# Gated Hedgehog attention with a SwiGLU gate: four FFN blocks computed ahead instead of six, and what lies around the hand-over from attention to FFN

## The chip, the cores and the metric

The kernel runs on one core of a Trainium2 chip, as one launch. The metric is the device time of the whole program in microseconds, the median of several runs. Beside these runs stands one profiled execution, from which all rows of the profile are taken; its span is the time from its first to its last recorded instruction.

The core has a matrix engine (TensorE, PE in the profile, with its weight loads as PEld), a vector engine (VectorE, DVE), a scalar engine (ScalarE, ACT), a general engine (GpSimd, POOL) and a queue engine that only issues transfers (SyncE, SP). Each executes its own instructions strictly in the order in which they stand. Work on different engines is tied together by semaphores: an instruction that waits holds up all that stand behind it on the same engine.

## What is computed

All data are float32. With 2048 rows, width 576, 32 heads of 18 and an FFN width of 4608, the reference is, cut to what matters:

```python
def A(x):                                     # linear attention with a learned feature map
    q, k, v = heads(x @ wqkv)
    pq, pk = q @ w_phi, k @ w_phi             # per head, 18 x 18
    phi_q = concat(softmax(pq), softmax(-pq)) # 36 features a head
    phi_k = concat(softmax(pk), softmax(-pk))
    kv, z = phi_k.T @ v, phi_k.sum(rows)
    return (phi_q @ kv) / (phi_q @ z + 1e-6) @ wo

def B(x):                                     # SwiGLU FFN
    return (silu(x @ w_gate) * (x @ w_up)) @ w_down

xn = layernorm(x)
out = x + A(xn) * silu(B(xn))
```

## The kernel before

**Arithmetic.** Each operand is split into a rounded part and a remainder, and a product is three matmuls: high by high, high by low, low by high. The split is the helper `split` (L57 to L59): a cast on ACT, then a subtraction on DVE that waits for it. The width of 576 is cut into chunks of 128 with a shared tail chunk, so that one 128 x 512 tile of a product with full depth takes 14 matmuls of 512 columns (`xw`, L82 to L92).

**Stages.** The order on each engine is set by a scheduler that places instructions by priority and by its own estimate of when operands are there; the program gives the sequence and marks some work as urgent (`tc.high_priority`) or as not before another instruction (`tc.issue_after`).

1. The rows are normalised and transposed into eight tiles `XB[i][j]`: for each half `i` of the rows two blocks of 512 rows by two halves of the width (L148 to L201). The feature map is folded into the query and key weights (`fold`, L210 to L220); the folded query weights are `QH` and `QL` in the pool `const`.
2. Key stage (L347 to L380): for 16 row tiles the key and value products, the softmaxes, and the sums `kv`. In the background `spread_out` (L325 to L343) forms sums and differences of the four tiles of each half of x and stores them in `sum_dram`, for the later FFN.
3. Query stage (L402 to L500): for eight blocks of 256 rows, `q_tile` (query product, softmaxes, denominators; the last DVE product of a row tile is kept in `last_e`), then a block later `numer` (five groups of heads: transposes into `pt`, a split to `ph` and `pl`, six matmuls into `po`, a split to `oh` and `ol`) and `project` (four quarters of 15 matmuls of 288 columns into `p`, each copied to `so` on ACT, L483; the store of `so` to `s_dram` from SP, L485). `po` and `p` have one buffer each. `tails` (L414 to L427) prepares the small tail weights of the FFN.
4. FFN. The F width is cut into 36 blocks of 128. For the first `EARLY` blocks, gate and up products are made plainly (`early_tile`, L110 to L121: for a half and a block 2 tiles x 2 weights x 14 matmuls = 56) and stored in `h_dram`. They stand behind the attention in the program (L502 to L505), and the scheduler sets their matmuls between those of the attention. The last early block is computed after the attention (L858 and after); between its two halves the sums of x are loaded into the tiles of the second half of x (`operands`, L511 to L530).
   The other blocks use a Strassen-like scheme (`gate_up`, L591 to L632): seven products of seven matmuls for a half and block, 49, from the operands `xo` and from weights that `gate_up_weights` (L532 to L564) loads into `ld`, combines on POOL (`ts`), splits into `w2` and `w1`, and stores for the second half of the rows in `w_dram`; `wt` holds the tails.
   The down product takes pairs of blocks, two pairs together, again in seven products (`strassen`, L730 to L809): `prep` (L799 to L806) splits the rows `h` to `hh` and the down weights to `dw`; part 0 are the products 1 and 7, part 1 are 4, 5, 6, 2, 3. The matmuls of the down product (`three`, L669) are placed between those of `gate_up` by `fill`. For the first group of the first half, the down weights of one pair come from `first_rows`, loaded into a part of `acc` (L860 to L862).
   `units` (L828 to L833) is the order of the 36 blocks for each half: an early block is put in at every fourth place and read back from `h_dram` (`stored`).

**Buffers.** Pools are laid on a stack: the FFN's weight pool `fw` (L507) takes the place that the attention's pools leave. A pool without more said waits, with its first use, for the pools whose place it takes; with `reuse_waits="tile"` each tile waits for just those that lay on its own bytes. `fp` and `fq` have that already.

**Queues.** Nearly all transfers are issued from SP, in one order; a transfer that has to wait for its data holds up those behind it.

Of the kernel before, what the change touches and what calls it, by code (L numbers as in the profile page):

```python
# [9 lines left out]
F32 = mybir.dt.float32  # L10
F32R = mybir.dt.float32r
# [5 lines left out]
S, D, H, DH, F = 2048, 576, 32, 18, 4608  # L17
P = 128
NT = S // P
BT = 512  # L20
# [3 lines left out]
HALF = D // 2  # L24
# [2 lines left out]
GROUPS = [(g * GW, min(GW, D - g * GW)) for g in range((D + GW - 1) // GW)]  # L27
NG = len(GROUPS)
QS = 256
EARLY = 6  # L30
TAILS = (NF - EARLY + 3) // 4
LAG = 3
RUSH = NF - 5
# [13 lines left out]
def gated_hedgehog_kernel(ctx: ExitStack, tc, x, w_qk, w_v, w_phi, wo, w_gu, w_tail, w_down, ident_in, mask_in, out):  # L47
# [5 lines left out]
    nc = tc.nc  # L53
# [56 lines left out]
    def early_tile(f, i, parts):  # L110
        for j in range(2):
# [8 lines left out]
                nc.vector.tensor_mul(h, pu, h)  # L120
            nc.sync.dma_start(h_dram[i, f, :, j * BT:(j + 1) * BT], h)  # L121

    with ExitStack() as att:
        const = att.enter_context(tc.tile_pool(name="const", bufs=1))
        ident = const.tile([P, P], F32, name="ident")
        nc.scalar.dma_start(ident, ident_in)
        QH = const.tile([P, 2, 3, D], F32R, name="QH")
        QL = const.tile([P, 2, 2, D], F32R, name="QL")
        mask = const.tile([GW, GH, DH], F32, name="mask")
        nc.scalar.dma_start(mask, mask_in)  # L130

        with ExitStack() as kst:
# [4 lines left out]
            with ExitStack() as pst:  # L137
# [104 lines left out]
                for n in range(6):  # L242
                    k, c = divmod(n, 3)
# [158 lines left out]
        with ExitStack() as qst:  # L402
# [66 lines left out]

            def project(b, oh, ol):  # L470
                for j in range(QS // P):
                    so = qk.tile([P, D], F32, name="so", bufs=1)
                    jc = slice(j * P, (j + 1) * P)
                    for i in range(2):
                        n = slice(i * HALF, (i + 1) * HALF)
                        ps = qps.tile([P, 512], F32, name="p")
                        k = 0
                        for g, (o, w) in enumerate(GROUPS):
                            for a, bw in ((oh, WOH), (oh, WOL), (ol, WOH)):
                                nc.tensor.matmul(ps[:, 0:HALF], a[0:w, g, jc], bw[0:w, g, n], start=k == 0,  # L480
                                                 stop=k == 3 * NG - 1)
                                k += 1
                        nc.scalar.copy(so[:, n], ps[:, 0:HALF])  # L483
                    r0 = b * QS + j * P
                    nc.sync.dma_start(s_dram[r0:r0 + P, :], so)  # L485

            order = list(range(S // QS // 2, S // QS)) + list(range(S // QS // 2))
            es, om = None, None
# [10 lines left out]
                with tc.issue_after(last_e[3 * n // 2 + 2].ins):  # L499
                    tails(n)  # L500

        for f, halves in [(0, (1,)), (1, (1, 0)), (0, (0,))] + [(f, (1, 0)) for f in range(2, EARLY - 1)]:  # L502
            parts = first_weights.pop(0) if first_weights else early_weights(f)
            for i in halves:
                early_tile(f, i, parts)  # L505

    fw = ctx.enter_context(tc.tile_pool(name="fw", bufs=1))  # L507
    fp = ctx.enter_context(tc.tile_pool(name="fp", bufs=1, reuse_waits="tile"))
    acc = fp.tile([P, 4, HT // 2, HALF], F32, name="acc")

    def operands(i):  # L511

        xo = [None] * 7
        for n in (0, 6, 1, 3, 5, 2, 4):
            if n < 3:
                j = (0, 1, 3)[n]
                if i:
                    t = xpool.tile([P, 5, BT], F32R, name=f"X0{j}")
                    nc.sync.dma_start(t.bitcast(F32), a_dram[n])
                else:  # L520
                    t = XB[0][j]
                xo[n] = [t[:, c] for c in range(5)]
                continue
            j = n - 3
            t = xpool.tile([P, 5, BT], F32R, name=f"X1{j}")
            nc.sync.dma_start(t.bitcast(F32).rearrange("p c n -> p (c n)"),
                              sum_dram[i, :, j].rearrange("p s c n -> p (s c n)"))
            v = t.rearrange("p c n -> p (c n)").rearrange("p (s c n) -> p s c n", s=4, c=5)
            xo[n] = [v[:, :, c] for c in range(5)]
        return xo  # L530

    def gate_up_weights(i, f):  # L532

        parts, wt = {}, fw.tile([96, 7, P], F32R, name="wt", bufs=2)
        n, q = divmod(f - EARLY, 4)
        if i == 0:
            ld = fw.tile([P, 2, D], F32, name="ld", bufs=2).rearrange("p a b -> p (a b)")
            ld = ld[:, 0:8 * P].rearrange("p (m c n) -> p m c n", m=4, c=2)
            nc.sync.dma_start(ld, w_gu[f, :, :, 0:2])
            ts = fw.tile([P, D], F32, name="ts")[:, 0:4 * P].rearrange("p (m c n) -> p m c n", m=2, c=2)  # L540

        def ready(m, src):
            k = 1 if m == 6 else 2
            w = fw.tile([P, k, 4, P], F32R, name=f"w{k}", bufs=2 if k == 1 else 4)
            if i:
                nc.sync.dma_start(w.bitcast(F32), w_dram[f - EARLY, :, m:m + k])
            else:
                split(w[:, :, 0:2], w[:, :, 2:4], src)
                if f < NF - 1:
                    nc.sync.dma_start(w_dram[f - EARLY, :, m:m + k], w.bitcast(F32))  # L550
            for c in range(k):
                parts[m + c] = w[:, c]

        ready(0, None if i else ld[:, 0:2])
# [90 lines left out]
    def late_finish(t):  # L645

        y = fw.tile([P, D], F32, name="ts")
        sx = fw.tile([P, 2, D], F32, name="ld", bufs=2)
        r = slice(t * P, t * P + P)
        nc.sync.dma_start(halves_of(y), y_dram[t])  # L650
        for m, src in enumerate((s_dram, xf)):
            nc.sync.dma_start(sx[:, m], src[r, :])
        nc.vector.tensor_mul(y, y, sx[:, 0])
        nc.vector.tensor_add(y, y, sx[:, 1])
        nc.sync.dma_start(of[r, :], y)
# [16 lines left out]
    def plain(i, fs, hr, final):  # L672

        ws = []

        def weights():
            raw = fw.tile([P, 2, D], F32, name="ld", bufs=2)
# [52 lines left out]
    def strassen(i, pairs, part, first):  # L730
# [65 lines left out]
        for f in ((p1, p7), (p4, p5, p6, p2, p3))[part]:  # L796
            hs, ws = [], []

            def prep(f=f, hs=hs, ws=ws):  # L799
                w2 = fq.tile([P, 2, 2, HALF], F32R, name="dw", bufs=3)  # L800
                with tc.issue_after(anchor[-1].ins) if first and i == 0 else ExitStack():
                    for n, g in enumerate(pairs):
                        h, w = f(g)
                        hs.append(split_h(h))
# [50 lines left out]

    todo = [(i, f) for i, n, f in units if f >= EARLY and (i == 0 or f < NF - 1)]
    kept = []
    parts = early_weights(EARLY - 1)  # L858
    early_tile(EARLY - 1, 1, parts)
    first_rows = [acc[:, 1].rearrange("p (a b) n -> p a (b n)", a=2)[:, n] for n in range(2)]  # L860
    for t, f in zip(first_rows, (EARLY, 0)):
        nc.sync.dma_start(t, w_down[f * P:(f + 1) * P, :])  # L862
    xo = operands(0)
    early_tile(EARLY - 1, 0, parts)
    ready = [gate_up_weights(*todo.pop(0))]
    est.close()
    fq = ctx.enter_context(tc.tile_pool(name="fq", bufs=1, reuse_waits="tile"))
# [73 lines left out]
```

## Time and profile before

| | us |
|---|---|
| median of 3 runs | 1649.47 |
| lowest and highest run | 1647.37, 1650.87 |
| profiled execution | 1648.95 |
| its span | 1647.0 |
| granted clock of TensorE, mean | 0.998 |

The profile's page gives busy time by engine, then groups of instructions by line: engine, operation, output <- inputs by the names in the program, shape and count, then busy time, mean length of one, and idle time of the engine just before them with what released it. Other views of the same trace are the timeline of an engine (start in us from the start of the span, length, line, operation, count of merged instructions, and in brackets the idle time before with its releaser), the waits by pairs of groups, and the busy time of each engine in chosen windows. Matmuls overlap in the pipeline, so the length of one is more than what it takes of the engine's time; the distance from start to start is that.

### The profile page before, as it was taken

What the parts mean: (1) busy time and instruction counts of PE and PEld (TensorE: products, weight loads), DVE (VectorE), ACT (ScalarE), POOL (GpSimd) and SP (SyncE); (2) the same over time, 40 slices, a digit from 0 to 9 for tenths busy, and PEclk for the clock granted to TensorE, in tenths of its full rate; (3) what the DMA queues carried; (4) which work ended last, traced back from release to release, by engine and by line L of the source; (5) the groups of instructions that cost most, each with busy time, mean ns of one, the idle gap of its engine ahead of it and who ended that gap; (6) DMA issues with size and microseconds to landing.
All of it is one profiled execution on the core that took longest, in us unless ns stands there. A gap on an engine that the chain in (4) does not pass through costs nothing.

```text
span 1647.0 us, 25211 instructions
## 1 busy us (share of the span) xinstructions
PE 1613.3 (98%) x9441; PEld 1436.0 (87%) x9441; DVE 1178.3 (72%) x1722; ACT 715.3 (43%) x1389; POOL 618.7 (38%) x660
## 2 busy tenths in 40 slices
PE   6999999999999999999999999999999999999998
PEld 5899998999987688888888888888888888888887
DVE  7677758989852476887887778844666677566578
ACT  5533345443431365444544445445433333333334
POOL 3467500343202344554554453422333244133132
PEclk9999999999999999999999999999999999999999
DMA  9623303343218545455455454495545556455435
GB/s 285 215 79 103 116 34 105 92 142 117 74 45 289 204 159 191 161 175 181 171 176 176 173 179 164 132 361 170 164 127 161 174 167 216 152 183 187 141 114 172
DMA packets 118107, 264.68 MB, mean 161 GB/s; under 512 B 12418, under 2 KB 48386, under 8 KB 116194
## 3 DMA queue, kind: packets, MB, share of 16 engines
q1 hardware_dynamic: 107628, 247.44, 45.0%
q0 software_dynamic: 3072, 11.02, 2.4%
q10 hardware_dynamic: 7286, 4.63, 0.9%
q8 instruction: 74, 1.21, 0.3%
q14 instruction: 47, 0.39, 0.1%
HBM read 164.21 MB, written 98.83 MB: 160 GB/s over the span
## 4 chain that ended last, share of the span: by engine, by line
PE 66%; DVE 2%; issue 1%; DMA 0%; POOL 0%; ACT 0%; SPq 0%; DVEq 0%; POOLq 0%
PE pd L669 24%; PE px L570 23%; PE pw L570 11%; PE py L570 6%; PE pe L92 2%; DVE acc L641 0%; DVE hh L59 0%; DMA hb<-h_dram 0%; DMA X<-s_dram 0%; DVE dw L59 0%; DVE w L59 0%; DVE ha L630 0%; DVE acc L642 0%; DVE s L604 0%; DVE acc L824 0%
## 5 line engine op out<-in xcount | busy, mean ns | idle before, releaser
L669 PEld LDWEIGHTS pd<-dw,hh 128*128 128x128 f32 x3048 | 431.9, 189 | 28.4 <-DVE dw L59 5.4
L669 PE MATMUL pd<-dw,hh 128*128 128x288 f32 x3048 | 448.3, 297 | 5.7 <-DVE dw L59 4.0
L570 PE MATMUL px<-X,w 128*128 128x512 f32 x1440 | 373.5, 393 | 1.5 <-ACT w L58 1.0
L570 PEld LDWEIGHTS px<-X,w 128*128 128x128 f32 x1440 | 261.3, 188 | 52.7 <-ACT s L599 3.5
L570 PE MATMUL pw<-X,w 128*128 128x512 f32 x720 | 185.5, 393 | 0.0
L570 PEld LDWEIGHTS pw<-X,w 128*128 128x128 f32 x720 | 134.7, 188 | 30.3 <-DVE s L604 0.3
L604 DVE TENSOR_TENSOR s<-pw,s 128x512 f32<-128x512 f32 x120 | 82.5, 687 | 102.6 <-ACT s L599 91.8
L92 PE MATMUL pe<-X,wh 128*128 128x512 f32 (+1 forms) x480 | 152.1, 400 | 1.7 <-POOL X L199 0.7
L794 DVE TENSOR_TENSOR acc<-pd,acc 128x576 f32<-128x576 f32 x128 | 96.1, 751 | 77.9 <-PE pd L669 77.8
L599 ACT COPY s<-px 128x512 f32<-128x512 f32 x120 | 70.3, 586 | 155.1 <-PE px L570 154.9
L59 DVE TENSOR_TENSOR hh<-ha,hh 128x512 fp32r<-128x512 f32 x140 | 115.5, 850 | 14.8 <-ACT hh L58 13.8
L58 ACT CAST hh<-ha 128x512 fp32r<-128x512 f32 x140 | 82.7, 619 | 95.4 <-PE pd L669 72.2
L92 PE MATMUL p<-KVWH,X 128*128 128x288 f32 (+1 forms) x640 | 123.6, 298 | 0.4 <-DVE phi L274 0.4
L766 POOL TENSOR_TENSOR hb<-hb 128x512 f32<-128x512 f32 x34 | 46.4, 1364 | 164.1 <-DVE hb L626 163.6
L92 PEld LDWEIGHTS pe<-X,wh 128*128 128x128 f32 (+1 forms) x480 | 88.5, 189 | 19.7 <-DVE h L120 1.5
L92 PEld LDWEIGHTS p<-KVWH,X 128*128 128x128 f32 (+1 forms) x640 | 100.5, 188 | 1.1 <-issue 0.8
L59 DVE TENSOR_TENSOR w<-ld,w 128x512 fp32r<-128x512 f32 (+1 forms) x90 | 76.2, 847 | 31.9 <-ACT w L58 30.5
L570 PE MATMUL px<-X,wt 96*128 96x512 f32 x240 | 94.8, 395 | 0.0
L570 PE MATMUL py<-X,w 128*128 128x512 f32 x360 | 94.0, 394 | 0.1
L779 POOL TENSOR_TENSOR ha<-ha 128x512 f32<-128x512 f32 x34 | 52.4, 1556 | 109.5 <-DVE hh L59 109.5
L58 ACT CAST w<-ld 128x512 fp32r<-128x512 f32 (+1 forms) x90 | 49.4, 549 | 87.5 <-POOL ld L560 55.2
L753 POOL TENSOR_TENSOR h<-ha,hb 128x512 f32<-128x512 f32 x34 | 45.4, 1334 | 100.7 <-DVE ha L630 66.6
(181 smaller groups left out, 3044.1 us busy)
## 6 DMA issues: line engine op xcount, KB each, us to landing
w_dram<-w SPq DMA_DIRECT2D x87, 512.0 KB, 2.8
w<-w_dram SPq DMA_DIRECT2D x87, 512.0 KB, 4.4
wt<-t_dram SPq DMA_DIRECT2D x59, 336.0 KB, 3.5
ld<-in_B_w_gu SPq DMA_DIRECT2D x30, 512.0 KB, 4.5
X<-sum_dram SPq DMA_DIRECT2D x8, 1280.0 KB, 6.8
rt<-in_B_w_down SPq DMA_DIRECT2D x33, 288.0 KB, 3.9
rb<-in_B_w_down SPq DMA_DIRECT2D x33, 288.0 KB, 4.0
w_dram<-w SPq DMA_DIRECT2D x29, 256.0 KB
```

The lines of the kernel that those rows point to most:

```text
L58: nc.scalar.copy(hi, src)
L59: nc.vector.tensor_sub(lo, src, hi)
L92: nc.tensor.matmul(ps, l, r, start=n == 0, stop=n == len(pairs) - 1)
L570: nc.tensor.matmul(ps, l, r, start=first and n == 0, stop=last and n == len(mm) - 1, skip_group_check=True)
L599: nc.scalar.copy(t, ps)
L604: nc.vector.tensor_add(t, ps, t)
L669: nc.tensor.matmul(ps, l, r, start=first and n == 0 and m == 0, stop=n == len(hs) - 1 and m == 2, skip_group_check=True)
L753: sub(s, g["h"][0][0], g["h"][0][1])
L766: nc.gpsimd.tensor_add(a21, a21, g["h"][1][1])
L779: sub(a12, a12, g["h"][0][0])
L794: nc.vector.tensor_add(a2, pd[:, :, 0:HALF], a2)
```

## The change

- `EARLY` is 4 for 6: blocks 0 to 3 are computed plainly, 4 to 35 by the Strassen-like scheme. The number of tail loads (`TAILS`) stays 8.
- The early work is issued in another order: half 1 of block 0, then blocks 1, 2 and 3 with both halves, then half 0 of block 0. None is left for after the attention. When half 1 of block 3 has been issued, `operands(0)` is: the loads of the x sums now stand inside the query stage, ahead of the last two early halves.
- `QH` and `QL` are allocated first in `const`. `fw` waits tile by tile. In it, `ld` and `wt` are two named buffers each, `ld0`, `ts` and `wt0` come first, so that they lie on the bytes of `QH`.
- `so` is half as wide with two buffers; each quarter of a projection is stored by its own transfer, issued from ACT.
- In `strassen`, only part 0 of the first group still waits for the last anchor (the last product of the FFN block before); part 1 does not.

```diff
@@
-EARLY = 6
+EARLY = 4
@@
+    def operands(i):
...
     with ExitStack() as att:
         const = att.enter_context(tc.tile_pool(name="const", bufs=1))
+        QH = const.tile([P, 2, 3, D], F32R, name="QH")
+        QL = const.tile([P, 2, 2, D], F32R, name="QL")
         ident = const.tile([P, P], F32, name="ident")
         nc.scalar.dma_start(ident, ident_in)
-        QH = const.tile([P, 2, 3, D], F32R, name="QH")
-        QL = const.tile([P, 2, 2, D], F32R, name="QL")
@@ project
                 for j in range(QS // P):
-                    so = qk.tile([P, D], F32, name="so", bufs=1)
                     jc = slice(j * P, (j + 1) * P)
+                    r0 = b * QS + j * P
                     for i in range(2):
...
-                        nc.scalar.copy(so[:, n], ps[:, 0:HALF])
-                    r0 = b * QS + j * P
-                    nc.sync.dma_start(s_dram[r0:r0 + P, :], so)
+                        so = qk.tile([P, HALF], F32, name="so", bufs=2)
+                        nc.scalar.copy(so, ps[:, 0:HALF])
+                        nc.scalar.dma_start(s_dram[r0:r0 + P, n], so)
@@
-        for f, halves in [(0, (1,)), (1, (1, 0)), (0, (0,))] + [(f, (1, 0)) for f in range(2, EARLY - 1)]:
+        for f, halves in [(0, (1,))] + [(f, (1, 0)) for f in range(1, EARLY)] + [(0, (0,))]:
             parts = first_weights.pop(0) if first_weights else early_weights(f)
             for i in halves:
                 early_tile(f, i, parts)
-
-    fw = ctx.enter_context(tc.tile_pool(name="fw", bufs=1))
+                if (f, i) == (EARLY - 1, 1):
+                    xo = operands(0)
+
+    fw = ctx.enter_context(tc.tile_pool(name="fw", bufs=1, reuse_waits="tile"))
@@
-    def operands(i):
...
     def gate_up_weights(i, f):
-        parts, wt = {}, fw.tile([96, 7, P], F32R, name="wt", bufs=2)
         n, q = divmod(f - EARLY, 4)
         if i == 0:
-            ld = fw.tile([P, 2, D], F32, name="ld", bufs=2).rearrange("p a b -> p (a b)")
+            ld = fw.tile([P, 2, D], F32, name=f"ld{f % 2}").rearrange("p a b -> p (a b)")
...
+        parts, wt = {}, fw.tile([96, 7, P], F32R, name=f"wt{f % 2}")
@@ strassen, prep
-                with tc.issue_after(anchor[-1].ins) if first and i == 0 else ExitStack():
+                with tc.issue_after(anchor[-1].ins) if first and i == 0 and part == 0 else ExitStack():
@@
     kept = []
-    parts = early_weights(EARLY - 1)
-    early_tile(EARLY - 1, 1, parts)
     first_rows = [acc[:, 1].rearrange("p (a b) n -> p a (b n)", a=2)[:, n] for n in range(2)]
     for t, f in zip(first_rows, (EARLY, 0)):
         nc.sync.dma_start(t, w_down[f * P:(f + 1) * P, :])
-    xo = operands(0)
-    early_tile(EARLY - 1, 0, parts)
     ready = [gate_up_weights(*todo.pop(0))]
```

The function `operands` is moved, not changed. `late_finish` and `plain` use the two named buffers `ld0` and `ld1` in place of the rotating `ld`.

More of the change, by code (lines that the diff above doesn't have):

```diff
@@ L121, in early_tile @@
             nc.sync.dma_start(h_dram[i, f, :, j * BT:(j + 1) * BT], h)
+    def operands(i):
+        xo = [None] * 7
+        for n in (0, 6, 1, 3, 5, 2, 4):
+            if n < 3:
+                j = (0, 1, 3)[n]
+                if i:
+                    t = xpool.tile([P, 5, BT], F32R, name=f"X0{j}")
+                    nc.sync.dma_start(t.bitcast(F32), a_dram[n])
+                else:
+                    t = XB[0][j]
+                xo[n] = [t[:, c] for c in range(5)]
+                continue
+            j = n - 3
+            t = xpool.tile([P, 5, BT], F32R, name=f"X1{j}")
+            nc.sync.dma_start(t.bitcast(F32).rearrange("p c n -> p (c n)"),
+                              sum_dram[i, :, j].rearrange("p s c n -> p (s c n)"))
+            v = t.rearrange("p c n -> p (c n)").rearrange("p (s c n) -> p s c n", s=4, c=5)
+            xo[n] = [v[:, :, c] for c in range(5)]
+        return xo
     with ExitStack() as att:
         const = att.enter_context(tc.tile_pool(name="const", bufs=1))
+        QH = const.tile([P, 2, 3, D], F32R, name="QH")
+        QL = const.tile([P, 2, 2, D], F32R, name="QL")
         ident = const.tile([P, P], F32, name="ident")
         nc.scalar.dma_start(ident, ident_in)
-        QH = const.tile([P, 2, 3, D], F32R, name="QH")
-        QL = const.tile([P, 2, 2, D], F32R, name="QL")
         mask = const.tile([GW, GH, DH], F32, name="mask")
@@ L505, in gated_hedgehog_kernel @@
                 early_tile(f, i, parts)
-    fw = ctx.enter_context(tc.tile_pool(name="fw", bufs=1))
+                if (f, i) == (EARLY - 1, 1):
+                    xo = operands(0)
+    fw = ctx.enter_context(tc.tile_pool(name="fw", bufs=1, reuse_waits="tile"))
     fp = ctx.enter_context(tc.tile_pool(name="fp", bufs=1, reuse_waits="tile"))
     acc = fp.tile([P, 4, HT // 2, HALF], F32, name="acc")
-    def operands(i):
[L513 to L530, printed above, removed]
     def gate_up_weights(i, f):
-        parts, wt = {}, fw.tile([96, 7, P], F32R, name="wt", bufs=2)
         n, q = divmod(f - EARLY, 4)
         if i == 0:
-            ld = fw.tile([P, 2, D], F32, name="ld", bufs=2).rearrange("p a b -> p (a b)")
+            ld = fw.tile([P, 2, D], F32, name=f"ld{f % 2}").rearrange("p a b -> p (a b)")
             ld = ld[:, 0:8 * P].rearrange("p (m c n) -> p m c n", m=4, c=2)
@@ L647, in late_finish @@
         y = fw.tile([P, D], F32, name="ts")
-        sx = fw.tile([P, 2, D], F32, name="ld", bufs=2)
+        sx = fw.tile([P, 2, D], F32, name=f"ld{t % 2}")
         r = slice(t * P, t * P + P)
@@ L676, in weights @@
         def weights():
-            raw = fw.tile([P, 2, D], F32, name="ld", bufs=2)
+            raw = fw.tile([P, 2, D], F32, name=f"ld{i}")
             for n, f in enumerate(fs):
```

## The prediction

> **What bounds the kernel now.** I read the page's first two parts, then TensorE cut into stages, then the stages' waits and the single instructions around the end of attention.
>
> ```profile
> span 1647.0 us, 25211 instructions
> PE 1613.3 (98%) x9441; PEld 1436.0 (87%) x9441; DVE 1178.3 (72%) x1722; ACT 715.3 (43%) x1389; POOL 618.7 (38%) x660
> ```
>
> TensorE (PE) has work for 98% of the span, so the time is its instructions plus its holes. The stages, by windows of busy time (columns: stretch, its length, busy time and count of PE, PEld, DVE, ACT, POOL, granted clock, DMA share, GB/s):
>
> ```profile
> 229.00:470.00 241.00, 238.38 (x1559) 215.77 (x1558) 209.78 (x334) 114.97 (x203) 63.60 (x128) 1.00 0.32 99
> 470.74:493.70 22.96, 22.96 (x145) 19.88 (x144) 7.26 (x14) 7.09 (x15) 0.00 (x0) 1.00 0.17 56
> 493.70:540.20 46.50, 46.18 (x198) 36.94 (x197) 11.01 (x15) 8.40 (x15) 9.05 (x11) 1.00 0.79 277
> 540.20:573.20 33.00, 29.82 (x122) 21.96 (x120) 16.04 (x20) 13.85 (x27) 14.70 (x15) 1.00 0.64 223
> 600.00:609.00 9.00, 6.54 (x42) 5.68 (x41) 8.38 (x9) 4.51 (x10) 6.02 (x6) 1.00 0.42 145
> 609.00:1600.00 991.00, 990.56 (x5455) 874.73 (x5455) 702.60 (x1008) 435.34 (x859) 389.99 (x351) 1.00 0.53 174
> 1600.00:1647.00 47.00, 39.74 (x233) 35.02 (x231) 38.14 (x49) 20.59 (x35) 12.78 (x6) 0.96 0.52 173
> ```
>
> In order: query stage; its last block, which only finishes the last two row tiles; a plain run of early matmuls with nothing else; the first two FFN blocks; the second group's down products; the dense FFN; the end. The dense FFN has 0.4 us of holes in 991, so what the change does there is a matter of matmul count alone. The prices, from the timeline of PE (start, length, x count; lengths overlap, so I take start to start):
>
> ```profile
> 249.90 0.86 PE L92 MATMUL pe<-X,wh 128*128 128x512 f32 x3
> 250.60 0.40 PE L92 MATMUL pe<-X,wl 128*128 128x512 f32 x1
> ...
> 488.59 0.35 PE L480 MATMUL p<-WOH,oh 126*128 126x288 f32 x1
> ...
> 490.50 0.29 PE L480 MATMUL p<-WOH,ol 72*128 72x288 f32 x1
> ...
> 540.21 0.40 PE L608 MATMUL py<-X,w 128*128 128x512 f32 x1
> ...
> 542.05 1.54 PE L570 MATMUL pw<-X,w 128*128 128x512 f32 x6
> ```
>
> A 512-column matmul takes 0.70/3 = 0.234 us early and (542.05-540.21)/8 = 0.23 us in the FFN; a 288-column one 1.91/14 = 0.135 us.
>
> **The change part by part.**
>
> *Two blocks fewer ahead.* An early block is 2 halves x 2 tiles x 2 weights x 14 = 112 matmuls; a later one 2 x 7 products x 7 = 98. Two blocks move over: 28 x 0.234 = **-6.6 us**. Later blocks add splits of weights, and 1.8 MB of them out and back each. On DVE, the fullest engine beside PE, the 30 blocks' splits are
>
> ```profile
> L59 DVE TENSOR_TENSOR w<-ld,w 128x512 fp32r<-128x512 f32 (+1 forms) x90 | 76.2, 847 | 31.9 <-ACT w L58 30.5
> ```
>
> or 2.5 us a block. DVE is busy 702.6 of the dense 991 us and the DMA engines 0.53, so I cost that at nothing; with no room on DVE it would be 2 x 2.5 us.
>
> *Where the early matmuls go.* By the order of instructions on PE, the query stage up to the last block holds 300 early matmuls for 298, so it stays as long. In the last block 6 remain for 35, and the 197 after the last projection are gone. What they covered in the last block (timelines of PE, ACT and DVE; idle before in brackets):
>
> ```profile
> 470.74 0.82 PE L460 MATMUL pt<-ident,e 128*126 128x128 f32 x6
> 471.31 0.70 PE L92 MATMUL pe<-X,wh 96*128 96x512 f32 x2
> ...
> 483.30 0.40 PE L466 MATMUL po<-ph,KVL 72*72 72x256 f32 x2
> 483.54 0.39 PE L466 MATMUL po<-pl,KVH 72*72 72x256 f32 x2
> 477.50 0.58 ACT L58 CAST ph<-pt 72x512 fp32r<-72x512 f32 x1 [1.81 <-PE po L466]
> 477.98 0.37 ACT L58 CAST oh<-po 126x256 fp32r<-126x256 f32 x1
> ...
> 488.09 0.40 ACT L483 COPY so<-p 128x288 f32<-128x288 f32 x1 [2.37 <-PE p L480]
> 476.06 0.41 DVE L59 TENSOR_TENSOR ol<-po,oh 126x256 fp32r<-126x256 f32 x1
> ```
>
> The five numerators share one `po` buffer, so each waits for the cast and the subtraction of the one before: 0.37 + 0.41 and about 0.3 of handing over between engines. Laid end to end after the transposes: first two groups 5.8 us as before, third 0.7 (6 matmuls at 0.12, start to start above), then 1.6 (with the 0.58 cast), 0.7, 1.1, 0.7: the last ends at 10.5 us instead of 483.9-470.7 = 13.2. The projection's first quarter ends 1.3 later; the other three are 15 x 0.135 = 2.05 each, and one `p` buffer puts a `so` copy (0.40, about 0.55 with handing over) ahead of each. A cast of `rt`, which now stands on ACT between two of these copies and waits for its load, adds about 0.4. End: 20 us after the transposes. Its work is 6 x 0.234 + 48 transposes (0.57/6 = 0.095) and numerator matmuls (0.12), 5.4, + 60 x 0.135 = 14.9 us, so 5.1 idle. Before: 22.96 - (35 x 0.234 + 13.5) = 1.2 idle. **+3.9 us**, between 0 (scheduler finds cover) and 8.2 (all 35 matmuls were cover).
>
> *Into the FFN.* Before, its first weights were split during the plain run. Now `ld0` lies over the query weights, so only its queue holds it: on SP it stands behind four loads of down weights, the first of which waits for the last numerator, 9.5 us ahead of the projection's end. Loads land as here (page, issues; and the first split before):
>
> ```profile
> ld<-in_B_w_gu SPq DMA_DIRECT2D x30, 512.0 KB, 4.5
> rt<-in_B_w_down SPq DMA_DIRECT2D x33, 288.0 KB, 3.9
> 498.57 0.62 ACT L58 CAST w<-ld 128x512 fp32r<-128x512 f32 x1 [4.39 <-DMA ld<-in_B_w_gu]
> 516.03 0.81 POOL L754 TENSOR_TENSOR td<-acc 128x288 f32<-128x288 f32 x1
> 72.60 0.93 ACTq L200 DMA_DIRECT2D x_dram<-xr  x2
> ```
>
> Four issues, then 4.5 and 1 to 2 for sharing: 7 to 8 us, in time. But on ACT the cast stands behind the last `so` copy and its new DMA issue: 0.4 + 0.46 + 0.62 and handing over make a hole of 1.75 us where there was 0.3: **+1.5** (0.7 to 3 if `ld0` is late).
>
> *First two blocks.* The order puts three casts of down weights on ACT ahead of the copy of `px` to `py`; they wait for `first_rows` (issued at the projection's end, 3.9 and an issue later) and two POOL subtractions of 0.8. The copy ends some 7 us after the projection, `py`'s product could start at 5.2: 2.1 idle. Against that, before, this stretch had 33.0 - 119 x 0.234 - 2 x 0.135 = 4.9 idle, with these waits:
>
> ```profile
> 564.05 1.66 PE L570 MATMUL px<-X,w 128*128 128x512 f32 x6 [0.54 <-ACT s L599]
> 568.06 0.50 PE L570 MATMUL px<-X,w 128*128 128x512 f32 x1 [0.52 <-ACT w L58]
> 573.22 0.66 PE L669 MATMUL pd<-dw,hh 128*128 128x288 f32 x3 [1.53 <-DVE dw L59]
> ...
> 601.11 3.51 PE L669 MATMUL pd<-dw,hh 128*128 128x288 f32 x25
> 605.53 0.66 PE L669 MATMUL pd<-dw,hh 128*128 128x288 f32 x3 [0.92 <-DVE dw L59]
> 606.04 0.62 PE L570 MATMUL px<-X,w 128*128 128x512 f32 x2
> 608.20 1.33 PE L669 MATMUL pd<-dw,hh 128*128 128x288 f32 x8 [1.54 <-DVE dw L59]
> ```
>
> Down weights cast early shorten the 1.53, and the wait for a weight cast falls into the `py` wait. I take **+0.4** (-1.5 to +2.1, and +4.5, one `ld`, if the second block's weights are late: `ld1` stands on SP behind four stores of split weights).
>
> *No anchor for the second down part.* The DVE halves of `dw` for the fourth product are, by the new order, ahead of the FFN block that held them; the waits at 605.53 and 608.20 are theirs. 600 to 609 has 9.0 us for 36 x 0.135 + 6 x 0.234 = 6.3: **-2.8** (0 if another split is late there).
>
> *x sums in the query stage.* The page's row of these loads:
>
> ```profile
> X<-sum_dram SPq DMA_DIRECT2D x8, 1280.0 KB, 6.8
> ```
>
> Four of them move on SP into the query stage, each waiting for the last early matmul that reads its buffer. Behind them stand loads of weight tails and stores of `h`; the next early tile but one waits for such a store. DMA share there is 0.32, and the first reader comes tens of us later. Nothing; a store held up by one load would cost up to 6.8.
>
> *`so` by halves from ACT.* 16 SP issues become 32 on ACT, 32 x 0.46 = 15 us on an engine busy 115 of 241. Queued behind each are casts of `ph` and `oh`, for which PE waits. Between 0 and 15; I take 0, because PE had 2.6 idle in 241 us there and 300 early matmuls stay as cover.
>
> Sum: -6.6 + 3.9 + 1.5 + 0.4 - 2.8 = **-3.6 us**, against the profiled execution's 1648.95 (span 1647.0 and 1.95 around it). The median shown, 1649.47, is 0.5 above it, so 1645.9.
>
> Against the change speaks the granted clock, if holes lower it: the 47 us at the end, with 7.3 idle, were granted 0.96, the stretch 540 to 573 with its holes 1.00. [...]
>
> **The rivals.**
>
> *Slower: ACT becomes the bound of the query stage.* From 15 of the 32 issues exposed, 15 x 0.46 = 6.9, the gain is a loss of 3.3. With 22 exposed: -3.6 + 10.1 = +6.5, 1656; with 15, 1652.8. For it: DVE busy 209.8 of 241 leaves the numerators' chain little slack. Against: ACT is under half busy. Chance 0.22.
>
> *No change: the FFN starts without its weights.* One `ld` exposed, +4.5: +0.9, 1650.4. For it: DMA share 0.79 when these loads ran before, and four stores stand ahead. Against: 8 us between issue and use. Chance 0.15.
>
> *More: the last block stays covered.* Without its +3.9: 1642. For it: ends of PE's waits are partly modelled; against: the one `po` buffer. Chance 0.12.
>
> *No change: the clock gives way in the last query block and the first FFN blocks.* The end's 4% over such a stretch of 47 us: +1.9, 1647.8. For it the end's row, against it the row at 540. Chance 0.04.
>
> **How the numbers follow.** Forecast 0.47. About 0.2% (3.3 us: under 1646.2, over 1652.8) is what measurement tells from no change; the forecast lies at that edge, and of its 0.47, spread over 1643 to 1648, 0.36 fall on faster and 0.11 on same. Faster: 0.36 + 0.12 (covered) = 0.48. Slower: 0.18 of the ACT rival and 0.07 of the late weights (more than one load late) = 0.25. Same: 0.11 + 0.04 + 0.08 + 0.04 = 0.27. Eight in ten: 1641.5, just below the covered case, to 1654, between 15 and 22 exposed issues.
>
> **What would show it.** PE's instructions 28 fewer; the last query block some 20 us with 5 idle on `ol` and `so`; a hole under 2 us before the first FFN matmul, released by ACT `w`; a wait on `py`; no `dw` wait in the second group; the dense FFN still without holes. Wrong, if the query stage up to the last block grows by over 2 us (ACT), if `px` waits for `w` in the second block over 2 us (loads), or if the clock is under 0.98 between 470 and 520.

## The result, and the profile after

| | before | after |
|---|---|---|
| median, us | 1649.62 (18 runs) | 1653.28 (18 runs) |
| lowest, highest | 1647.37, 1651.81 | 1651.01, 1655.21 |
| ratio after to before, 95% interval | | 1.0023, 1.0015 to 1.0030 |
| span of the profiled execution | 1647.0 | 1651.4 |

The change makes the kernel 3.7 us slower; in the profiled executions the difference is 4.4. The page after, its span and TensorE's line of busy time:

```profile
span 1651.4 us, 25210 instructions
PE 1608.6 (97%) x9413; PEld 1431.7 (87%) x9413; DVE 1180.3 (71%) x1730; ACT 726.6 (44%) x1407; POOL 628.2 (38%) x668
```

TensorE has 28 instructions fewer and 4.7 us less to do, and still ends 4.4 later: some 9 us of new holes. (Busy time also holds 1.7 us of a slower clock, shown below.) To find them I cut both traces at the same places in the program: the first instruction of the query stage, the first transposes of its last block, the first FFN matmul, the first down matmuls that wait for `dw`, the second `px` product behind them (5.7 us later before, 10.6 after), and the last 47 us. Windows after, then three of before (columns as in the prediction; before, the query stage from its first instruction is 241.60 us long, and the first two FFN blocks are those of the prediction's row, 33.0):

```profile
228.19:467.66 239.47, 239.02 (x1562) 217.15 (x1561) 207.96 (x330) 116.54 (x203) 65.93 (x128) 1.00 0.38 118
467.66:489.89 22.23, 17.77 (x116) 14.92 (x114) 6.01 (x12) 7.72 (x18) 2.14 (x3) 1.00 0.41 131
489.89:527.05 37.16, 30.35 (x119) 21.52 (x120) 18.10 (x24) 15.06 (x29) 18.66 (x21) 1.00 0.78 265
527.05:537.63 10.58, 5.80 (x33) 4.77 (x33) 7.68 (x10) 3.96 (x9) 7.39 (x8) 1.00 0.31 120
537.63:1604.40 1066.77, 1065.73 (x5805) 937.56 (x5806) 733.96 (x1058) 469.52 (x924) 410.11 (x370) 1.00 0.53 174
```

```profile
470.74:540.21 69.47, 69.15 (x342) 56.82 (x340) 18.27 (x29) 15.49 (x30) 9.05 (x11) 1.00 0.58 204
...
573.22:578.95 5.73, 5.73 (x34) 5.04 (x34) 4.99 (x8) 3.39 (x8) 3.29 (x4) 1.00 0.13 52
578.95:1600.00 1021.05, 1018.14 (x5606) 898.47 (x5605) 722.48 (x1034) 453.24 (x895) 403.92 (x364) 1.00 0.53 174
```

With 0.234 us a matmul, after less before, stage by stage:

| stage | length, us | matmuls by the program | left over, us | forecast |
|---|---|---|---|---|
| up to the query stage | -0.95 | 0 | -1.0 | 0 |
| query stage | -2.13 | +2 | -2.6 | 0 |
| last query block, into the FFN | -47.24 | -226 | +5.6 | +5.4 |
| first two FFN blocks | +4.15 | 0 | +4.2 | +0.4 |
| the next products | +4.85 | 0 | +4.9 | 0 |
| the rest | +45.72 | +196 | -0.1 | -2.8 |

The 28 matmuls fewer are -6.6 us, and the left-over column adds 11. Nine of these stand in the first 48 us of the FFN, for which 0.4 was forecast. The timeline of PE there (idle before in brackets, with what ended it):

```profile
489.89 0.50 PE L610 MATMUL py<-X,w 128*128 128x512 f32 x1 [1.50 <-ACT w L58]
495.37 1.65 PE L572 MATMUL py<-X,w 128*128 128x512 f32 x6 [1.45 <-ACT py L613]
499.54 1.67 PE L572 MATMUL px<-X,w 128*128 128x512 f32 x6 [0.68 <-ACT s L601]
502.56 0.49 PE L572 MATMUL px<-X,w 128*128 128x512 f32 x1 [1.11 <-ACT w L58]
...
527.05 0.67 PE L671 MATMUL pd<-dw,hh 128*128 128x288 f32 x3 [1.11 <-DVE dw L59]
529.62 1.33 PE L671 MATMUL pd<-dw,hh 128*128 128x288 f32 x8 [1.44 <-DVE dw L59]
537.63 2.73 PE L572 MATMUL px<-X,w 128*128 128x512 f32 x6 [3.34 <-ACT s L601]
```

The last and longest names `s`, the copy by which `snap` takes a running sum out of `px`. The copy itself needs 0.58 us. Why was it late? ACT's timeline, and below it POOL's, of the same microseconds:

```profile
536.14 0.43 ACT L58 CAST dw<-td 128x288 fp32r<-128x288 f32 x1 [3.48 <-POOL td L763]
536.48 0.61 ACT L58 CAST w<-ld 128x512 fp32r<-128x512 f32 x1
537.00 0.58 ACT L601 COPY s<-px 128x512 f32<-128x512 f32 x1
```

```profile
532.50 0.83 POOL L559 TENSOR_TENSOR ts<-ld 128x256 f32<-128x256 f32 x1 [2.34 <-issue]
533.40 1.06 POOL L560 TENSOR_TENSOR ts<-ld,ts 128x256 f32<-128x256 f32 x1
534.42 0.94 POOL L561 TENSOR_TENSOR ld<-ld 128x256 f32<-128x256 f32 x1
535.32 0.79 POOL L763 TENSOR_TENSOR td<-td,acc 128x288 f32<-128x288 f32 x1
```

PE waits for `s`; `s` stands on ACT behind a cast of down weights; that cast waits for the subtraction `td` on POOL; and `td` stands on POOL behind three subtractions for the next block's weights. ACT then sits 3.48 us with an instruction ready to run behind one that is not. In the kernel before the same `td` ran ahead of those three subtractions. It could not have run at once here either, because it overwrites a tile that one DVE subtraction of part 0 (which the anchor still holds) reads first (in the kernel before, POOL waits 2.33 us for that reading):

```profile
532.28 0.45 DVE L59 TENSOR_TENSOR dw<-td,dw 128x288 fp32r<-128x288 f32 x1
```

That ends at 532.73, so the three subtractions on POOL delay `td` by 2.6 us; the hole of PE is 3.34.

A second cost follows the hole. Windows of after around it; the seventh number is the granted clock:

```profile
533.00:537.60 4.60, 1.29 (x10) 1.03 (x8) 2.77 (x4) 1.46 (x4) 3.78 (x5) 1.00 0.29 117
537.60:541.00 3.40, 3.37 (x9) 2.71 (x10) 2.20 (x5) 2.21 (x6) 0.00 (x0) 0.54 0.67 197
541.00:544.00 3.00, 3.00 (x19) 2.76 (x18) 0.69 (x1) 1.05 (x2) 0.00 (x0) 0.95 0.64 225
```

After 4.6 us in which PE was busy 1.29, the clock was 0.54 for 3.4 us: 0.46 x 3.4 + 0.05 x 3 = 1.7 us. They stand in the table's last row, where the gone `dw` waits of the second group (2.5 us before, none after) had to show.

### The profile page after: what moved, and what is told of

Same layout as the page of the kernel before. It is cut to its first block, busy times and chain, and to the rows that moved or that the text cites. A ratio compares the mean times of both kernels' runs of the same rounds, so it can differ in the third digit from the quotient of the medians.

```text
span 1651.4 us, 25210 instructions
## 1 busy us (share of the span) xinstructions
PE 1608.6 (97%) x9413; PEld 1431.7 (87%) x9413; DVE 1180.3 (71%) x1730; ACT 726.6 (44%) x1407; POOL 628.2 (38%) x668
## 4 chain that ended last, share of the span: by engine, by line
PE 65%; DVE 1%; POOL 1%; DMA 1%; issue 1%; ACT 0%; SPq 0%; DVEq 0%; ACTq 0%
PE px L572 24%; PE pd L671 23%; PE pw L572 12%; PE py L572 6%; DVE acc L643 0%; DMA rb<-in_B_w_down 0%; DVE w L59 0%; DMA X<-s_dram 0%; DVE hh L59 0%; DVE acc L644 0%; POOL ld L562 0%; DVE s L606 0%; DVE acc L826 0%; DVE ha L632 0%; POOL hb L768 0%
## 5 line engine op out<-in xcount | busy, mean ns | idle before, releaser
L572 PE MATMUL px<-X,w 128*128 128x512 f32 x1536 | 399.3, 394 | 6.6 <-ACT s L601 5.2
L572 PEld LDWEIGHTS px<-X,w 128*128 128x128 f32 x1536 | 279.4, 189 | 62.6 <-ACT s L601 9.2
L572 PE MATMUL pw<-X,w 128*128 128x512 f32 x768 | 198.3, 393 | 0.8 <-DVE s L606 0.8
L572 PEld LDWEIGHTS pw<-X,w 128*128 128x128 f32 x768 | 143.5, 188 | 33.4 <-DVE s L606 1.5
L606 DVE TENSOR_TENSOR s<-pw,s 128x512 f32<-128x512 f32 x128 | 88.1, 688 | 105.5 <-ACT s L601 93.6
L59 DVE TENSOR_TENSOR hh<-ha,hh 128x512 fp32r<-128x512 f32 x140 | 107.6, 794 | 19.6 <-ACT hh L58 18.1
L92 PE MATMUL pe<-X,wh 128*128 128x512 f32 (+1 forms) x320 | 101.8, 400 | 1.3 <-POOL X L220 0.6
L572 PE MATMUL py<-X,w 128*128 128x512 f32 x384 | 100.0, 394 | 2.3 <-ACT py L613 2.3
L572 PE MATMUL px<-X,wt 96*128 96x512 f32 x256 | 101.2, 396 | 0.0
L613 ACT COPY py<-px 128x512 f32<-128x512 f32 x64 | 36.6, 572 | 106.2 <-PE px L572 79.3
```

The source lines that it names most:

```text
L59: nc.vector.tensor_sub(lo, src, hi)
L92: nc.tensor.matmul(ps, l, r, start=n == 0, stop=n == len(pairs) - 1)
L572: nc.tensor.matmul(ps, l, r, start=first and n == 0, stop=last and n == len(mm) - 1, skip_group_check=True)
L606: nc.vector.tensor_add(t, ps, t)
L613: nc.scalar.copy(yp, xp)
```

## The experiments

All ratios are to the kernel before, run beside each on the same chip; the chips differ between groups of experiments, and the median of the kernel before lies between 1649.2 and 1649.6 on them. Each trace is one execution.

| | edit | median, us | ratio, 95% interval |
|---|---|---|---|
| x1 | after, anchor back for part 1 | 1658.1 | 1.0050, 1.0037 to 1.0062 |
| x2 | before, part 1 without anchor | 1646.97 | 0.9984, 0.9975 to 0.9993 |
| x3 | before, `so` by halves from ACT | 1648.99 | 1.0001, 0.9992 to 1.0010 |
| x4 | after, EARLY = 5 | 1646.19 | 0.9978, 0.9970 to 0.9987 |
| x5 | after, next load ahead of stores | 1655.52 | 1.0036, 1.0024 to 1.0049 |
| x6 | x4 and x5 together | 1645.93 | 0.9982, 0.9973 to 0.9991 |
| x7 | after, EARLY = 6 | 1643.54 | 0.9968, 0.9956 to 0.9981 |
| x8 | after, no anchor at all | 1647.11 | 0.9988, 0.9979 to 0.9997 |
| x9 | x7, no anchor at all | 1645.85 | 0.9982, 0.9973 to 0.9991 |
| x10 | x7, `so` whole from SP | 1648.47 | 0.9999, 0.9991 to 1.0008 |
| x11 | after, EARLY = 7 | 1648.48 | 0.9998, 0.9989 to 1.0006 |

### Is it the removed anchor? (x1, x2)

The cast that blocks ACT belongs to part 1, which the change had released. That was the first suspect.

```diff
-                with tc.issue_after(anchor[-1].ins) if first and i == 0 and part == 0 else ExitStack():
+                with tc.issue_after(anchor[-1].ins) if first and i == 0 else ExitStack():
```

> The changed kernel with one edit undone: part 1 of the first group's down products waits for the anchor again. In the changed kernel's trace PE waits 3.34 us at 537.63 for a snap copy that stands on ACT behind a cast of down weights (dw<-td) that waits for POOL, and the stretch around it takes 10.6 us where before it took 5.7. Theory A (the removed anchor let those casts in too early, and they turned into this wait): the 4.85 us go, the two dw waits of the second group (2.5 us) come back, 1653.3 - 4.85 + 2.5 = 1651 us, ratio to the kernel before 1.001. Theory B (the FFN starts with no weights in hand, each next load stands on SP behind stores of split weights, and the late POOL work is its last effect; the anchor has no part in it): the 3.3 us wait stays at its place, the 2.5 us come back, 1655.8 us, ratio 1.0038.

x2 makes the opposite edit in the kernel before.

> The kernel before with only the anchor edit: part 1 of the first group's down products waits for no anchor. As predicted, the waits at 605.53 and 608.20 go and 2.8 us with them: 1649.6 - 2.8 = 1646.8, ratio 0.9983; theory B says the same, 1647.1, since there the weights are in hand. Theory A: the casts come too early here as well, 4.85 lost and 2.5 gained, 1652, ratio 1.0014.

Theory A is out on both. With the anchor back the changed kernel is 4.8 us slower still; without it the kernel before gains 2.5, close to the prediction's term of 2.8. Theory B had the direction right in both, but x1 came out 2.3 us above its 1655.8. x1's timeline of PE:

```profile
538.40 1.65 PE L572 MATMUL px<-X,w 128*128 128x512 f32 x6 [1.81 <-ACT s L601]
...
565.51 0.66 PE L671 MATMUL pd<-dw,hh 128*128 128x288 f32 x3 [0.92 <-DVE dw L59]
```

The wait for `s` is still there, and the second group's `dw` waits are back. The wait is 1.81 us and not 3.34 because PE came to it late with its own work: the clock had already dropped to a mean of 0.66 between 530 and 535. The copy itself was no earlier to speak of: the product starts 47.28 us after the first FFN matmul, where after has 47.74. Behind the `dw` waits of 0.92 and 1.54 us the clock falls to 0.60 (windows of x1):

```profile
565.00:568.00 3.00, 1.12 (x5) 0.69 (x5) 3.00 (x3) 1.44 (x4) 2.84 (x4) 1.00 0.24 98
568.00:571.00 3.00, 2.83 (x11) 2.64 (x12) 3.00 (x4) 0.64 (x1) 2.92 (x3) 0.60 0.00 0
```

### Does `so` from ACT cost anything? (x3)

```diff
-                    so = qk.tile([P, D], F32, name="so", bufs=1)
...
-                        nc.scalar.copy(so[:, n], ps[:, 0:HALF])
...
-                    nc.sync.dma_start(s_dram[r0:r0 + P, :], so)
+                        so = qk.tile([P, HALF], F32, name="so", bufs=2)
+                        nc.scalar.copy(so, ps[:, 0:HALF])
+                        nc.scalar.dma_start(s_dram[r0:r0 + P, n], so)
```

> The kernel before with only the store of so changed: halves with two buffers, each stored from ACT. The prediction cost this at nothing (1649.6, ratio 1.000), its rival at 7 to 10 us more (1656 to 1660). What the changed kernel's trace suggests: its query stage is 2.1 us shorter with two matmuls more and has no wait for so, so 1649.6 - 2.5 = 1647, ratio 0.9985, with no PE wait for so in the query stage.

No cost and no gain, to within some 1.7 us. The prediction's slower rival, ACT as the bound of the query stage, is out. The gain that the trace of after suggested failed too: the waits for `so` are gone, but PE waits 2.5 us for `e` in the same stage. That is in x3's waits (total, times, longest); the profiled execution took 1654.2 us, where the median is 1649.0:

```profile
PE p L92 <- DVE e L274: 2.5, 2, 1.3
```

These waits for `e` were 0.4 us in after and 1.8 in x1, two kernels with the same order in that stage. So a microsecond of the table's -2.6 is chance.

### Is it the number of early blocks? (x4, x7, x11)

```diff
-EARLY = 4
+EARLY = 5
```

> The changed kernel with EARLY = 5. By the order of instructions 69 early matmuls stand in the last query block and 57 behind the last projection, where the changed kernel has 18 and none. 14 matmuls more than the changed kernel, +3.3 us. Theory B (what is lost is the cover: early matmuls that fill the last block's holes and hide the first loads and splits): the last block's idle 4.5 us goes, most of the hole and of the 4.2 us in the first two blocks and of the 4.85 us after them go too, 1653.3 + 3.3 - 4.5 - 1.5 - 7 = 1643.5, ratio 0.9963. Theory A (the anchor): the 4.85 stay, 1653.3 + 3.3 - 4.5 - 1.5 = 1650.5, ratio 1.0005, with a wait for s of over 3 us behind the first down products.

> The changed kernel with EARLY = 6 as before: all edits but the number of early blocks. 69 early matmuls stand in the last query block and 169 behind the last projection. Theory B (only the missing cover costs): as the kernel before without the anchor, 1647, ratio 0.9985, and no FFN hole over 1 us beyond those of before. Rival theory D (one of the other edits, the layout of ld over the query weights or the x sums in the query stage, costs by itself): 1650 or more, ratio 1.0003 or above.

> All edits with EARLY = 7: 281 early matmuls behind the last projection for 169. Fourteen matmuls more, 3.3 us, and no cover to gain if 169 are enough: 1643.5 + 3.3 = 1646.8, ratio 0.9985. If the first FFN blocks still lack lead at six: at or under 1643.5. The step from five to six gained 2.7 and from four to five 7.1 us, each against 3.3 us of matmuls.

The same edits with 4, 5, 6 and 7 early blocks: 1653.3, 1646.2, 1643.5, 1648.5 us. A block more costs 3.3 us of matmuls; from 4 to 5 it pays back 10.4 us, from 5 to 6 6.0, from 6 to 7 nothing. (The intervals of five and six overlap, so which of them is faster is less sure than that both beat four.) With six, the other edits together gain 5.7 us on the kernel before, and this is the fastest kernel of the study. What the early matmuls behind the last projection (0, 57 and 169 with four, five and six blocks) bought shows in PE's waits behind that point. x4, then x7:

```profile
PE py L572 <- ACT py L613: 1.8, 1, 1.8
PE px L572 <- ACT s L601: 1.6, 3, 0.9
PE pd L671 <- DVE dw L59: 1.5, 1, 1.5
PE px L572 <- ACT w L58: 1.0, 2, 0.5
```

```profile
PE pd L671 <- DVE dw L59: 1.5, 1, 1.5
PE px L572 <- ACT w L58: 1.0, 2, 0.5
PE px L572 <- ACT s L601: 0.5, 1, 0.5
```

Neither has a hole in the last query block or ahead of the first FFN matmul. The seventh block's price came out at 4.9 us instead of 3.3, and where the rest went is not shown: in that profile `e` cost 1.9 us (0.5 with six) and a `wt` load 0.6.

### Are the loads late by their place on SP? (x5, x6)

`load` is the load of `ld`, cut out of `gate_up_weights`; the first block's `wt` goes ahead of it.

```diff
             ld = loaded.pop(f) if f in loaded else load(f)
+        if i == 0 and f + 1 < NF:
+            loaded[f + 1] = load(f + 1)
...
         ready(0, None if i else ld[:, 0:2])
```

> The changed kernel with one thing moved: on SP the load of the next block's weights (ld) is issued ahead of the stores of this block's split weights instead of behind them, and wt of the first block ahead of both. In the changed kernel the second block's load is issued at 493.9, 5.6 us after the last projection, and lands at 501.9; here some 4 us earlier. Theory B1 (what is late in the first blocks are loads, and they are late by their place on SP): the waits for w and s in the second block (1.11 + 0.27 + 0.98) go, and the 3.34 us at the third with the 1.7 us of lower clock behind it: 1653.3 - 2.4 - 3.3 - 1.7 = 1646, ratio 0.998. Theory B2 (the loads are not the limit; the chain of splits over ACT, DVE and POOL through one ts, or full DMA engines, share 0.98 between 490 and 500, is): under 1 us better, 1652.5, ratio 1.0018.

> Both edits: EARLY = 5 and the load of the next block ahead of the stores. With five early blocks alone (1646.2 us) the second block still waits 0.9 + 0.2 us for s, and py 1.83 us, since its load lands at 516, 2 us after the first FFN matmul. Theory B1: 2 to 3 us of these go, 1643.5 us, ratio 0.9964, and this is the fastest so far. Theory B2: as with five blocks alone, 1646, ratio 0.998.

B1 is out: there is no gain with four blocks (2.2 us slower, with intervals that overlap) and none with five. The second block's load did go out at 488.6 instead of 493.9, and yet PE met a hole of the same size earlier (x5, timelines of PE, ACT and POOL):

```profile
502.34 2.29 PE L584 MATMUL px<-X,w 128*128 128x512 f32 x6 [3.23 <-ACT s L613]
```

```profile
494.35 0.61 ACT L58 CAST w<-ld 128x512 fp32r<-128x512 f32 x1
499.87 0.40 ACT L58 CAST w<-ld 128x256 fp32r<-128x256 f32 x1 [4.91 <-POOL ld L574]
...
501.71 0.57 ACT L613 COPY s<-px 128x512 f32<-128x512 f32 x1
```

```profile
491.89 0.81 POOL L768 TENSOR_TENSOR td<-acc 128x288 f32<-128x288 f32 x1 [0.76 <-DMA acc<-in_B_w_down]
...
495.69 1.26 POOL L774 TENSOR_TENSOR td<-rb,rt 128x288 f32<-128x288 f32 x1
496.91 0.74 POOL L571 TENSOR_TENSOR ts<-ld 128x256 f32<-128x256 f32 x1
```

The weights were there at 494.35, when ACT cast their first part. POOL then worked off six subtractions of down weights before it came to them, ACT waited 4.91 us at the cast of their combination, and `s` stood behind. The load came earlier, and the hole only moved. This gave theory P: the start of the FFN is bound by the chain of preparation over POOL, ACT and DVE, and by where its pieces stand in the queues.

### Is it the place of the down weights' preparation? (x8, x9)

```diff
-                with tc.issue_after(anchor[-1].ins) if first and i == 0 and part == 0 else ExitStack():
+                with ExitStack():
```

> The changed kernel with no anchor for either part of the first group's down products. By the order of instructions the two POOL subtractions td<-td and the two ACT casts dw<-td of the fourth product then stand in the first FFN block; in the changed kernel they stand in the third, where the subtractions wait for the anchored DVE half of part 0 that reads the same td, the casts wait for the subtractions, and the snap copy behind them makes PE wait 3.34 us. Theory P (the start of the FFN is bound by this chain of preparation on POOL, ACT and DVE and by where its pieces stand in the queues, not by loads): the 3.34 us and the lower clock behind it (1.7 us) go, and the dw waits of 1.11 and 1.44 us too: 1653.3 - 3.3 - 1.7 - 2.5 = 1646 us, ratio 0.998. Theory Q (whatever is moved ahead only delays the splits of the second block's weights by its own length; two subtractions of 0.8 and two casts of 0.43 more stand ahead of them): 2.5 us lost again, and the time stays within 1.5 us of the changed kernel, 1652 to 1655, ratio 1.0015 to 1.003.

> The fastest kernel so far (all edits, but EARLY = 6: 1643.5 us) with no anchor for either part. Its profile still has one dw wait of 1.5 us in the first group. Theory P: that wait goes, since under the 169 plain early matmuls there is time for the preparation: 1642 us, ratio 0.9955. Theory Q: a snap copy or the py copy waits for the casts moved ahead of it, 1.5 us or more, 1643.5 to 1645, ratio 0.9965 to 0.9975.

x8 gains 6.2 us on the changed kernel with the same four blocks, the same matmuls and the same loads; theory Q's bound does not hold here. Its timeline of ACT and of PE:

```profile
500.97 0.43 ACT L58 CAST dw<-td 128x288 fp32r<-128x288 f32 x1 [3.33 <-POOL td L763]
...
502.57 0.58 ACT L601 COPY s<-px 128x512 f32<-128x512 f32 x1
```

```profile
503.20 1.66 PE L572 MATMUL px<-X,w 128*128 128x512 f32 x6 [2.02 <-ACT s L601]
...
534.15 1.64 PE L572 MATMUL px<-X,w 128*128 128x512 f32 x6 [0.89 <-ACT s L601]
```

The casts now wait in the first block, where they delay `s` by 2.02 us (0.68 in after). But the product that began 47.74 us into the FFN in after begins at 534.15 - 492.13 = 42.02 us, and the clock stays at 1.00 there (in each 5 us from 525 to 555). From there to the end x8 takes 1.6 us less, about what the lower clock cost in after.

x9 shows the other side. With six blocks the same edit removes the `dw` wait of 1.5 us, and puts one of the casts ahead of a snap copy, where it waits for POOL (ACT, then PE):

```profile
550.93 0.43 ACT L58 CAST dw<-td 128x288 fp32r<-128x288 f32 x1 [4.39 <-POOL td L763]
551.27 0.58 ACT L601 COPY s<-px 128x512 f32<-128x512 f32 x1
```

```profile
551.90 2.27 PE L572 MATMUL px<-X,w 128*128 128x512 f32 x6 [3.25 <-ACT s L601]
```

That is the very pair of after's 3.34 us. It is slower than x7 by 2.3 (intervals that overlap a little): here the mechanism that theory Q named held, at a price a little above its bound, and P's 1642 failed. The anchor of part 0 is thus neither good nor bad by itself. In these traces what counts is where a cast that waits for POOL stands ahead of a snap copy, and how long it waits there.

### And `so`, with six blocks? (x10)

The edit is x3's the other way round, in x7.

> All edits with EARLY = 6, but so stored whole from SP as before. Before, the query stage has two waits for so of 1.2 to 1.3 us together; with halves there is none. If the halves gain what the waits show: 1643.5 + 1.3 = 1644.8, ratio 0.9973. If they gain nothing, as in the kernel before with halves alone (ratio 1.0001): 1643.5, ratio 0.9965, and the gain of the kernel with six blocks beyond the anchor's 2.7 us comes from elsewhere. If 32 issues cost ACT something: under 1642.5.

1648.5: the halves are worth some 5 us here, more than expected and against x3. The waits of x10 in the query stage and its last block, and ACT at the longest:

```profile
PE p L501 <- ACT so L504: 4.2, 3, 1.9
```

```profile
495.55 0.40 ACT L504 COPY so<-p 128x288 f32<-128x288 f32 x1 [4.67 <-DMA s_dram<-so]
```

One whole `so` must be stored before the next row tile's first copy; in the last block that store is waited for 4.67 us on ACT and 1.89 on PE, and over 495 to 500 the clock is a mean of 0.66, at most another 0.34 x 5 = 1.7 us. Together with the other waits for `so` that is up to 5.9 us. Two half buffers stored from ACT take it away (x7 has no wait for `so`). Why x3 saw none of it is argued, not shown. In x10, SP issues the 512 KB load of `ld` at 491.32, 0.41 us behind this store at 490.91, which the new place of `ld` over the query weights allows. In the kernel before no such load follows the store there, and PE waits for `so` 1.2 us in all. x10 does not separate the width of the buffer from the queue of the store. It also leaves 186 early matmuls behind the last projection where x7 has 169, so that the last block has fewer to fill its waits.

## Why the prediction was wrong, point by point

- *Two blocks fewer ahead, -6.6.* Right: 28 PE instructions fewer, and x11, 4.9 us slower for one block more, does not speak against the 3.3 a block. That the later blocks' splits cost nothing holds for the dense FFN only.
- *Last query block and into the FFN, +3.9 and +1.5.* Right: +5.6 together. From the transposes to the end of the last projection 20.7 us (20 forecast), and the hole ahead of the first FFN matmul is 1.50 us, released by ACT's `w` (1.75 forecast).
- *First two blocks, +0.4 (-1.5 to +2.1).* **This step failed:** +4.2, and +4.9 in the third block, which it did not follow. It named the right queue (the wait for `py` is 1.45 where 2.1 was said), but took the idle 4.9 of before as something that the change would shorten, and `ld1`'s lateness as one isolated bound of 4.5. Before, the plain run of 197 early matmuls was also the time in which the first two blocks' weights were loaded, combined and cast (ACT at 498.57 to 516) and POOL's first three subtractions for the down weights ran (from 516.03). Without it all of that runs just in time, on engines that take it in one order, and late pieces hold up the copies out of `px` (ACT stood 3.48 us at such a piece in after, 4.91 in x5). That the lost time is the cause x4 and x7 show by giving it back; that the order on ACT and POOL decides how much is lost x8 shows by another order alone, at the same four blocks.
- *No anchor for the second down part, -2.8.* Right in its own place: no `dw` wait in the second group, 2.5 us gained in the kernel before (x2), 4.8 in the changed kernel (x1 undoes it). The working asked which waits go, not which instructions the released casts now stand ahead of, and what those casts wait for.
- *x sums in the query stage, 0.* Nothing in the query stage points to a cost (it is 2.1 us shorter with two matmuls more); not tried by itself.
- *`so` from ACT, 0 to 15, taken as 0.* Right as to cost (x3); an issue on ACT took 0.33 us and not 0.46. That the stores by halves can gain 5 us (x10) was missed.
- *Clock gives way, +1.9, chance 0.04.* It did, by 1.7 us, in another place: not in the last query block with its gaps of 0.26 to 0.57 us, but behind the 3.34 us, where the clock was 0.54. The sign named for it (a clock under 0.98 between 470 and 520) did not come: it was 1.00.
- *ACT becomes the bound of the query stage, 1652.8 to 1656.* The time came out in this rival's bounds, by another mechanism: the query stage did not grow. That 1653.3 lies below the 1654 of the prediction's range is luck too, for that end was drawn from issues exposed on ACT, and x3 shows no cost of them. *FFN without its weights:* `ld1` was late by 1.11 us, and x5 shows that the loads were not the limit.

What stays open: x10, with all edits at six blocks but the halves of `so`, is 1.5 us slower (2.5 by the ratios) than x2, the kernel before without part 1's anchor. So the layout, the order of the early work and the place of the x sums together gain nothing there, and may cost; they were not tried one by one. Also open is whether an order exists in which four early blocks beat six; x8 with its 1647.1 is the nearest tried.

## What to carry to other kernels

Work that "only fills" between two stages is also the time in which the next stage's preparation runs: before taking it away, follow that preparation through its engines, each in the order of its instructions (ACT's 3.48 us in after), until the steady state, not just to the first matmul. Where an order constraint is dropped, look up for each released instruction what it waits for and what short copy that the critical engine needs now stands behind it. An edit's worth can depend on its neighbours: letting part 1 go without its anchor gained 2.5 us in the kernel before and 4.8 in the changed one, and letting part 0 go too gained 6.2 with four early blocks and lost 2.3 with six.

## What the runs showed of the hardware

The granted clock fell after holes of PE in some places and not in others of the same size. After 4.6 us with PE busy for 1.29 it fell to 0.54 for 3.4 us in after (537.6 to 541); after 3.0 us with PE busy for 1.12, cut into waits of 0.92 and 1.54, it fell to 0.60 in x1. The same two waits in the kernel before, with the same 1.12 us of work, left it at 1.00:

```profile
605.20:608.20 3.00, 1.12 (x6) 0.70 (x6) 3.00 (x4) 1.27 (x4) 2.88 (x3) 1.00 0.15 60
608.20:611.20 3.00, 3.00 (x16) 2.67 (x17) 3.00 (x3) 1.12 (x2) 2.92 (x3) 1.00 0.02 5
```

With waits of 1.12 and 1.45 us near 530 in x1 it was 0.66 over 530 to 535; with 1.11 and 1.44 in after it was 1.00 over the same window. With one wait of 1.89 us, which ended at 496.00, it was 0.66 over 495 to 500 in x10; with one of 2.02 in x8, which ended at 503.20, it stayed at 1.00 from 490 to 510. The window of x10:

```profile
495.00:500.00 5.00, 4.00 (x17) 3.95 (x18) 0.00 (x0) 0.63 (x2) 2.15 (x3) 0.66 0.02 8
```

By one less the clock, times the length of the windows, such a drop cost about 1.7 us on top of the hole in after, at most that in x10, and about that twice in x1 (0.34 x 5, and 0.40 x 3 + 0.17 x 3 with the 0.83 over 571 to 574). Runs with a lower mean clock took longer: of 77 runs of the kernel before, those with a mean clock of 0.997 took 1650.5 us on average (19 runs), those with 0.998 took 1649.5 (32) and those with 0.999 took 1648.2 (26).
